# Attention ahead of two MoE layers: float32 scores in the two row halves of the array, one block for both heads' last queries, memory read by token

## The chip, the cores and the metric

The kernel runs on one core of one Trainium2 chip. The metric is the device time of one execution in microseconds, from inputs in HBM to the output in HBM; several executions are timed and the median is given. One more execution is recorded by the hardware profiler, and every line number (L381 is line 381 of the kernel) and every duration of the profile is from it.

## The reference

Attention with a causal mask over 4 batches of 8 heads, 576 tokens of 64 features each, mixed with a read from a memory matrix; then two layers of a feed-forward network over the 2304 tokens.

```
scores = q k^T / 8, masked above the diagonal
a      = exp(scores - max) / (sum + 1e-9)          local = a v
q_p    = phi(q),  phi(x) = max(x, 0) + exp(min(x, 0))
mem    = (q_p M_prev) / (q_p z_prev + 1e-6)        # per head
x      = g * mem + (1 - g) * local,  g = sigmoid(beta) per head
h = x w_in;  x = (h - tanh(h)) w_out                # first layer, 512 -> 2048 -> 512
h = x w2_in; e = h softmax(h); x = (layernorm(e) g_ln) w2_out   # second, 512 -> 1024 -> 512
```

The MoE weights arrive as 64-bit floats; the kernel builds 32-bit ones from the two words of each.

## The kernel before

The work has three stages: attention (class `Attention`), the first layer (`Moe1`) and the second (`Moe2`). Attention treats two heads at once, a pair: the 64 features of one head lie on partitions 0 to 63 and those of the other on 64 to 127. There are 16 pairs. Each token block c has 128 queries that are moved up by 64, so that five blocks of 64, 192, 320, 448 and 576 keys cover a head (`s_mm`, L289).

- q and k of a pair are loaded (L127, L131) and transposed on TensorE (L154, L155).
- **Scores.** The matmuls run in the type float32r, which keeps fewer bits, so q and k are both split into a high and a low part: `q_hi`, `q_lo` (L169), `q_mv` and `k_hi` (L203), `k_lo` (L213), `k_hd`, `k_ld` (L182 on an engine, L184 as a DMA). Each head's q tile stacks the high part on one partition half and the low part on the other, and each k part lies twice, on both halves. One matmul of 128 rows then adds two of the products; KH and KL give the rest.
- **Softmax.** `s_max` (L303, DVE) adds the mask and takes the maximum, `s_exp` (L319, ACT) the exponential with the row sum, `s_inv` (L331, DVE) 1/sum, and `s_norm` (L336, POOL) multiplies by it and by 1 - g.
- **Memory.** phi is made from the untransposed q on DVE and ACT, `f_z` and `f_red` (L241, L245) form the denominator, `f_scale` (L264, POOL) multiplies phi by g and its inverse, `f_t` and `f_ev` transpose it, and `a_mem` (L359) puts the product with M into the PSUM tile X.
- **Product with v.** The probabilities are transposed in four groups a head (`a_t`, L381; `GROUPS` lists key block and query block), copied out of PSUM (`a_ev`, L387), and `a_pv` (L400) adds their product with v to X, one head in each column half of the array. `x_ev` (L415) copies X out and `x_mv` (L420) stores it by DMA into xT, which the first layer reads.

PSUM has three kinds of tile: "S" (two buffers of 1024 columns), "T" (two of 512) and "X" (one of 1024).

**The order of the work is written out by hand.** Inside the manual schedule each engine, and the DMA queue of SyncE, issues in the order of emission. `PROLOGUE` lists the operations of the first two pairs; `PERIOD` is one loop turn, in which `k_t:1` means the transposes of k of the next pair, `s_mm:-1:-:3` block 3 of the head before. A letter names the engine of a copy. `run` goes through them; at the operations called `room`, work on the MoE weights and on xT is let in (`Between`, L633: the class hands out one step at a time). Its first job is added after the first operation that `run` yields, and a job starts by fetching two blocks of raw weights (L688). Once the last scores are done, each attention operation on TensorE is preceded by four matmuls of the first layer (the filler, L589).

```
        for p in range(self.START, NP - last):
            for j, (name, at, engine, part) in enumerate(ops):
                ...
                    if p >= NP and name.startswith(self.ON_PE):
                        next(filler, None)
                    emit(name, i, engine, part)
                yield p, j
```

Of the kernel before, what the change touches and what calls it, by code (L numbers as in the profile page):

```python
# [19 lines left out]
NCB = 4  # L20


class Attention:
# [3 lines left out]
    NPB = 4  # L27

    def __init__(self, ap, sp, ps, tc, q, k, v, M_prev, z_prev, beta, xT, ident):
# [12 lines left out]
        self.NC = S // P + 1  # L42
        assert S == 576 and D == 64
        NC = self.NC

# [4 lines left out]
        self.mask = sp.tile([P, S], F32, tag="mask", name="mask", bufs=1)  # L50
        nc.gpsimd.memset(self.mask, 0.0)
        nc.gpsimd.affine_select(
            out=self.mask[:, S - P :],
            in_=self.mask[:, S - P :],
            compare_op=ALU.is_ge,
            fill=-8.0e9,
            base=0,
            pattern=[[-1, P]],
            channel_multiplier=1,
        )  # L60

        self.nat, self.Qs, self.Pt, self.Md = {}, [], [], []
        for i in range(2):
            t = sp.tile([P, NC, 2, D], F32, tag=f"q{i}", name=f"q{i}", bufs=1)
            nc.gpsimd.memset(t[D:P, NC - 1], 0.0)
            self.nat["q", i] = t

        for name, pool, n, free in (("k", sp, 2, slice(D, P)), ("v", ap, 3, slice(0, D))):
            for i in range(n):
                t = pool.tile([P, NC, 2, D], F32, tag=f"{name}{i}", name=f"{name}{i}", bufs=1)  # L70
                nc.gpsimd.memset(t[free, NC - 1], 0.0)
                self.nat[name, i] = t
        for i in range(2):
            t = ap.tile([P, self.HP, P], F32, tag=f"Md{i}", name=f"Md{i}", bufs=1)
            nc.gpsimd.memset(t, 0.0)
            self.Md.append(t)
        for i in range(4):
            t = sp.tile([P, D + S], F32R, tag=f"Qs{i}", name=f"Qs{i}", bufs=1)
            nc.gpsimd.memset(t[:, 0:D].bitcast(F32), 0.0)
            self.Qs.append(t)  # L80
        self.poff = [P * i * (i + 1) // 2 for i in range(NC)]
        for i in range(self.NPB):
            t = ap.tile([P, self.poff[NC - 1] + S], F32, tag=f"P{i}", name=f"P{i}", bufs=1)
            for c in range(NC - 1):
                o = self.poff[c + 1]
                nc.gpsimd.memset(t[:, o - D : o], 0.0)
            self.Pt.append(t)
        for name in ("x", "zb", "ql", "T", "St", "K", "e", "f", "n", "fT", "mx", "sm", "sc", "pt"):
            setattr(self, name, {})


    def load_gate(self):
# [26 lines left out]

    def _load(self, p, t, src, order, last=0):  # L120
# [3 lines left out]
        full = P * (NC - 1)  # L124
# [21 lines left out]
    def _transposed(self, name, t):  # L146


        nc, NC, S = self.nc, self.NC, self.S
        T = self.ps.tile([P, 1024], F32, tag="S", name=name, bufs=2)  # L150
        full = P * (NC - 1)
# [10 lines left out]
    def q_hi(self, p):  # L162

        self.copy(self.Qs[2 * p % 4][:, self.D :], self.T["q"])

    def q_lo(self, p):
        L = self.ql[p] = self.sp.tile([P, self.S], F32R, tag="ql", name=f"ql{p}", bufs=1)
        H = self.Qs[2 * p % 4][:, self.D :]
        self.nc.vector.tensor_tensor(L, self.T["q"], H.bitcast(F32), ALU.subtract)  # L169

    def q_mv(self, p, i):

        Q = [self.Qs[(2 * p + j) % 4][:, self.D :] for j in range(2)]
        L = self.ql[p]
        a, b = self._half(0)
        out, in_ = ((Q[1][b], Q[0][b]), (Q[0][b], L[a]), (Q[1][a], L[b]))[i]
        self._move(out, in_.bitcast(F32))

    def _move(self, out, in_):

        if self.copy:
            self.copy(out, in_)  # L182
        else:
            self.nc.sync.dma_start(out=out.bitcast(F32), in_=in_)  # L184

    def _half(self, j):

        D = self.D
        a, b = slice(0, D), slice(D, P)
        return (b, a) if j else (a, b)  # L190
# [5 lines left out]
    def k_hi(self, p, j):  # L196

        a, b = self._half(j)
        KH, KL = self.K[2 * p + j] = [
            self.sp.tile([P, self.S], F32R, tag=t, name=f"{t}{p}_{j}", bufs=4)  # L200
            for t in ("KH", "KL")
        ]
        self.copy(KH[a], self.T["k"][a])  # L203

    def k_hd(self, p, j):
        a, b = self._half(j)
        KH, _ = self.K[2 * p + j]
        self._move(KH[b], KH[a].bitcast(F32))

    def k_lo(self, p, j):  # L210
        a, b = self._half(j)
        KH, KL = self.K[2 * p + j]
        self.nc.vector.tensor_tensor(KL[a], self.T["k"][a], KH[a].bitcast(F32), ALU.subtract)  # L213

    def k_ld(self, p, j):
        a, b = self._half(j)
        _, KL = self.K[2 * p + j]
        self._move(KL[b], KL[a].bitcast(F32))


    def f_neg(self, p):
        e = self.e[p] = self.ap.tile([P, self.NC, 2, self.D], F32, tag="fe", name=f"e{p}", bufs=1)
        flat = "p c j d -> p (c j d)"
        self.nc.vector.tensor_scalar_min(e.rearrange(flat), self.nat["q", p % 2].rearrange(flat), 0.0)

    def f_pos(self, p):
        f = self.f[p] = self.ap.tile([P, self.NC, 2, self.D], F32, tag="f", name=f"f{p}", bufs=2)
        flat = "p c j d -> p (c j d)"
        self.nc.vector.tensor_scalar_max(f.rearrange(flat), self.nat["q", p % 2].rearrange(flat), 0.0)

    def f_exp(self, p):
        e = self.e[p].rearrange("p c j d -> p (c j d)")
        self.nc.scalar.activation(e, e, AF.Exp)

    def f_sum(self, p):
        self.eng.tensor_tensor(self.f[p], self.f[p], self.e[p], ALU.add)

    def f_z(self, p):
        b, h0 = divmod(2 * p, self.H)
        z = self.zb[b][:, h0 // 2].unsqueeze(1).broadcast_to([P, self.NC, 2, self.D])  # L240
        self.nc.gpsimd.tensor_tensor(self.e[p], self.f[p], z, ALU.mult)  # L241

    def f_red(self, p):
        n = self.n[p] = self.ap.tile([P, self.NC, 2], F32, tag="fn", name=f"n{p}")
        self.nc.vector.tensor_reduce(n, self.e[p], AX.X, ALU.add)  # L245
# [877 lines left out]
```

## Time and profile before

| | |
|---|---|
| median of three runs | 868.15 us (867.0 to 870.17) |
| the profiled execution | 866.64 us, of which the profile's span is 864.8 us |
| TensorE busy | 837.6 us, 97% of the span |
| DVE, ACT, POOL busy | 625.1, 395.8, 366.7 us |
| mean granted TensorE clock | 0.998 |
| start of the first layer's second product (Y, L616) | 250.47 us |

Busy time of TensorE counts an instruction until its results are out, and the next one starts before that, so 97% doesn't say that the array works at its peak. How much work a stretch of TensorE holds is read from start to start. PEld is TensorE's loading of weights, which overlaps its matmuls. Attention ends, for the purpose of this text, where the first Y of L616 starts.

### The profile page before, as it was taken

How to read it: one execution, taken by the hardware profiler on the slowest of the kernel's cores; microseconds unless marked ns; L12 is line 12 of the kernel's file. 1: busy time of each engine (PE TensorE's matmuls, PEld its weight loads, DVE VectorE, ACT ScalarE, POOL GpSimd, SP SyncE). 2: the span in 40 equal slices, each digit the busy share in tenths (PEclk: the TensorE clock that was granted, in tenths of full speed). 3: DMA queues.
4: the chain of work that ended last, by engine and by line, in shares of the span. 5: the costliest groups of instructions: out<-in, count | busy, mean ns of one | idle time of the engine just before them, and what ended most of it. 6: DMA issues, size and time to landing. Idle time of an engine off the chain costs nothing.

```text
span 864.8 us, 13784 instructions
## 1 busy us (share of the span) xinstructions
PE 837.6 (97%) x5016; PEld 752.5 (87%) x5016; DVE 625.1 (72%) x1215; ACT 395.8 (46%) x843; POOL 366.7 (42%) x453
## 2 busy tenths in 40 slices
PE   4999999999999899999999999999999999999998
PEld 3777777777789899999999999999998888888887
DVE  6888889988657877787777877775787655555553
ACT  5898888888744323323233232332322323323222
POOL 6968787887835333333333333430533111111110
PEclk9999999999999999999999999999999999999999
DMA  6896677565110211212112121220200000000001
GB/s 131 198 207 161 161 183 164 146 146 135 45 52 25 74 60 63 74 50 74 54 69 74 49 74 49 74 70 5 72 27 0 25 25 25 20 19 25 25 25 37
DMA packets 82372, 64.66 MB, mean 75 GB/s; under 512 B 63296, under 2 KB 63552, under 8 KB 82304
## 3 DMA queue, kind: packets, MB, share of 16 engines
q1 hardware_dynamic: 82304, 63.78, 27.3%
q8 instruction: 40, 0.66, 0.3%
q14 instruction: 28, 0.23, 0.1%
HBM read 40.90 MB, written 4.72 MB: 53 GB/s over the span
## 4 chain that ended last, share of the span: by engine, by line
PE 73%; DVE 1%; ACT 1%; issue 0%; ACTq 0%
PE Y L616 23%; PE H L589 23%; PE H L796 11%; PE T L835 2%; PE X L400 1%; PE T L381 1%; PE O9X L865 1%; PE O3X L865 1%; PE O13X L865 1%; PE O11X L865 1%; PE O7X L865 1%; PE O5X L865 1%; PE O1X L865 1%; PE O0X L865 1%; PE O15X L865 1%; PE O16S L865 1%
## 5 line engine op out<-in xcount | busy, mean ns | idle before, releaser
L616 PE MATMUL Y<-G,wo 128*128 128x384 f32 x1152 | 209.3, 337 | 3.0 <-DVE yT L628 2.2
L616 PEld LDWEIGHTS Y<-G,wo 128*128 128x128 f32 x1152 | 202.2, 189 | 3.6 <-ACT cva L732 2.5
L589 PE MATMUL H<-xh,wi 128*128 128x384 f32 x768 | 150.7, 337 | 0.0
L589 PEld LDWEIGHTS H<-xh,wi 128*128 128x128 f32 x768 | 134.8, 188 | 1.3 <-issue 0.8
L600 ACT ACTIVATE t<-H 128x768 f32<-128x768 f32 x48 | 39.1, 814 | 197.4 <-PE H L589 193.0
L750 POOL TENSOR_TENSOR cvw<-cvw,cva 128x512 f32<-128x512 f32 x44 | 56.8, 1291 | 164.6 <-DVE cva L748 121.9
L336 POOL TENSOR_SCALAR P<-P,sm,og 128x192 f32<-128x192 f32 (+4 forms) x160 | 105.8, 673 | 23.1 <-DVE sm L331 19.7
L319 ACT ACTIVATE P<-sc,mx 128x192 f32<-128x192 f32 (+4 forms) x160 | 88.8, 558 | 9.1 <-DVE mx L303 8.6
L796 PE MATMUL H<-w2i,Ys 128*128 128x512 f32 x384 | 90.0, 390 | 0.0
L796 PEld LDWEIGHTS H<-w2i,Ys 128*128 128x128 f32 x384 | 72.0, 188 | 15.0
L601 DVE TENSOR_TENSOR t<-H,t 128x768 f32<-128x768 f32 x48 | 45.9, 957 | 51.6 <-ACT t L600 51.6
L381 PEld LDWEIGHTS T<-ident,P 128*128 128x128 f32 x480 | 52.4, 141 | 35.0 <-DVE mx L303 11.1
L589 PE MATMUL H<-xT,wi 128*128 128x384 f32 x384 | 82.8, 337 | 0.0
L303 DVE CUSTOM_DVE_ANT_0 sc<-S,mask 128x64 f32<-128x64 f32 (+4 forms) x160 | 73.1, 486 | 11.5 <-PE S L289 9.1
L381 PE MATMUL T<-ident,P 128*128 128x128 f32 x480 | 73.2, 281 | 7.6 <-DVE mx L303 6.2
L630 DVE TENSOR_TENSOR yT<-Y,yT 128x384 f32<-128x384 f32 (+1 forms) x126 | 79.0, 683 | 0.0
L603 DVE TENSOR_TENSOR G<-t,G 128x768 fp32r<-128x768 f32 x48 | 46.3, 965 | 42.4 <-ACT G L602 42.4
L824 POOL TENSOR_TENSOR s<-s,nhalf 128x1 f32<-128x1 f32 x18 | 9.9, 551 | 153.3 <-DVE s L823 134.5
L602 ACT CAST G<-t 128x768 fp32r<-128x768 f32 x48 | 40.1, 835 | 63.6 <-DVE t L601 63.6
L589 PEld LDWEIGHTS H<-xT,wi 128*128 128x128 f32 x384 | 67.9, 188 | 0.1
L807 DVE TENSOR_REDUCE s<-H 128x1 f32<-128x1024 f32 x18 | 22.0, 1224 | 59.9 <-PE H L796 59.9
L289 PE MATMUL S<-KH,Qs 128*128 128x256 f32 (+3 forms) x192 | 56.2, 330 | 8.2 <-DVE Qs L182 5.3
(285 smaller groups left out, 1427.0 us busy)
## 6 DMA issues: line engine op xcount, KB each, us to landing
raw<-in_moe_w_in_dram SPq DMA_DIRECT2D x24, 512.0 KB, 3.7
raw<-in_moe_w_out_dram SPq DMA_DIRECT2D x24, 512.0 KB, 3.5
xT<-x SPq DMA_DIRECT2D x16, 288.0 KB, 2.4
out_dram<-ob SPq DMA_DIRECT2D x17, 256.0 KB, 2.0
KH<-KH SPq DMA_DIRECT2D x30, 144.0 KB, 2.8
KL<-KL SPq DMA_DIRECT2D x30, 144.0 KB, 2.7
q<-in_q_dram SPq DMA_DIRECT2D x16, 256.0 KB, 3.7
k<-in_k_dram SPq DMA_DIRECT2D x16, 256.0 KB, 3.6
```

Of the source, the lines that this page charges most:

```text
L289: nc.tensor.matmul(t[:, o + a : o + z], lh, K[:, a:z], start=(i == 0), stop=(i == 1), skip_group_check=True,)
L303: self.nc.vector.tensor_tensor_reduce(out=sc, in0=t[:, o : o + W], in1=self.mask[:, self.S - W :], scale=-0.125, scalar=3.0e38, op0=ALU.ad ...
L319: self.nc.scalar.activation(self._p(n, c), self.sc[c], AF.Exp, bias=self.mx[n][:, c : c + 1], scale=-1.0, accum_out=self.sm[n][:, c : c + 1],)
L336: self.nc.gpsimd.tensor_scalar(d, d, self.sm[n][:, c : c + 1], self.og[:, h : h + 1], ALU.mult, ALU.mult)
L381: nc.tensor.transpose(T[:, at : at + P], Pt[:, col : col + P], self.ident)
L589: nc.tensor.matmul(H[:, f], wi[:, wl, c, f * P : (f + 1) * P], self.x[n][xl][:, c], start=(i == 0), stop=(i == 3 * KD - 1),)
L603: nc.vector.tensor_tensor(G[:, 1], t, G[:, 0].bitcast(F32), ALU.subtract)
L616: nc.tensor.matmul(Y[d][:, 0:NB], wo[:, wl, f, d * P : (d + 1) * P], G[:, gl, f], start=(i == 0), stop=(i == 3 * KF - 1),)
L630: nc.vector.tensor_tensor(y, src, y, ALU.add)
L750: self.eng.tensor_tensor(w, w, a, ALU.add)
L796: nc.tensor.matmul(H[:, nh * 512 : (nh + 1) * 512], Y[:, yl, c, :], w2i[:, wl, c, nh * 512 : (nh + 1) * 512], start=(k == 0), stop=(k == 3 ...
L865: nc.tensor.matmul(O, L[:, ll, f, :], self.w2o[f][:, wl, a : a + w], start=(f == 0 and k == 0), stop=(f == KF - 1 and k == 2),)
```

## The change

Only the attention class changes, and with it the order of its operations; the MoE stages, the filler and the weight conversion stay.

- **Scores** are plain float32 matmuls on the transposed q and k, which are copied out of PSUM whole (`q_ev`, `k_ev`). A head has 64 features, so its matmul uses 64 of the array's 128 rows; head 0 takes rows 0 to 63, head 1 rows 64 to 127. The splits and their moves go. Blocks are no longer moved up: four blocks of 128 queries with 128 to 512 keys (`s_r`).
- **The last 64 queries** of both heads share one tile of 128 partitions (`s_l`): head 0 on partitions 0 to 63, head 1 on 64 to 127, with a mask and a gate of their own. Softmax has nine blocks a pair where it had ten.
- **Memory by token.** phi is made from the transposed q and used as the stationary operand: `m_mm` multiplies it with one tile that holds M of both heads and z as two more columns (`MZ`, 130 columns, g already multiplied in by `m_gate`). `m_eps`, `m_inv` and `m_mul` divide on DVE, and `a_mem` lays the result into X by five transposes.
- **Product with v.** The probabilities are transposed in five groups of four blocks and one of five for the last queries; `PV` lists the products. X has 640 columns, of which the store skips 64.
- **The order.** `PROLOGUE` is empty, the loop starts two periods early, and `PERIOD` is new. M and z of a batch are loaded inside it.

```
+    MW, MS = 130, 176
...
-    def q_hi(self, p):
-    def q_lo(self, p):
-    def q_mv(self, p, i):
-    def k_hi(self, p, j):
-    def k_hd(self, p, j):
-    def k_lo(self, p, j):
-    def k_ld(self, p, j):
+    def q_ev(self, p):
+        t = self.QT[p] = self.sp.tile([P, self.S], F32, tag="QT", name=f"QT{p}", bufs=2)
+        self.copy(t, self.T["q"])
...
+    def load_m(self, p):
...
+            nc.sync.dma_start(
+                out=t[rows, :, P + j : P + j + 1],
+                in_=self.z[b].rearrange("(c j) (d o) -> j d c o", j=2, o=1)[j],
+            )
...
+    def m_mm(self, p):
...
+        for i in range(self.NC):
+            at = min(P * i, self.S - P)
+            o = self.MS * i
+            nc.tensor.matmul(
+                R[:, o : o + self.MW], f[:, at : at + P], self.MZ[b % 2][:, c, :], start=True, stop=True,
+                skip_group_check=True,
+            )
...
+    def s_r(self, p, c):
+        nc, D = self.nc, self.D
+        Q, K = self.QT[p], self.KT[p]
+        if c == 1:
+            t = [
+                self.ps.tile([P, 512], F32, tag="T", name=f"S{p}_{c}{j}", bufs=2)
+                for j in range(2)
+            ]
+        else:
+            S = self.ps.tile([P, 1024], F32, tag="S", name=f"S{p}_{c}", bufs=2)
+            t = [S[:, 0:512], S[:, 512:1024]]
...
+        for r, o in ((c, 0),) if c > 1 else ((1, 0), (0, 256)):
+            w = P * (r + 1)
+            for j in range(2):
+                rows = slice(j * D, (j + 1) * D)
+                s = self.St[p, 2 * r + j] = t[j][:, o : o + w]
                 nc.tensor.matmul(
+                    s, Q[rows, P * r : P * r + P], K[rows, 0:w], start=True, stop=True,
                     skip_group_check=True,
                 )
+    def s_l(self, p):
...
+        for a, z in ((0, full), (full, S)):
+            for j in range(2):
+                rows = slice(j * D, (j + 1) * D)
+                nc.tensor.matmul(
+                    t[rows, a:z], Q[rows, full:S], K[rows, a:z], start=True, stop=True,
+                    skip_group_check=True,
+                )
...
+    PV = [
+        [(0, 0, 512, (0, 1), (0, 0))],
+        [(1, 128, 384, (2, 3), (0, 0)), (3, 384, 128, (2, 3), (384, 384))],
+        [(2, 256, 256, (4, 4), (0, 256))],
+        [(kb, 576, 64, (5, 5), (P * kb, P * kb + 64)) for kb in range(5)],
+    ]
...
     PERIOD = """
+        load_q:2:- f_exp:0:- s_exp:0:-:5 s_r:0:-:3 s_max:0:-:0 s_norm:-1:-:5 a_pv:-2:-:3
+        s_max:0:-:1 s_norm:-1:-:6 s_max:0:-:2 s_exp:0:-:0 x_mv:-3:- a_pv:-2:-:2
+        s_max:0:-:6 s_norm:-1:-:8 s_exp:0:-:1 s_max:0:-:7 s_norm:-1:-:7 a_pv:-2:-:1
+        a_pv:-2:-:0 s_max:0:-:3 m_gate:1:- s_l:0:- a_t:-1:-:2 s_exp:0:-:2 s_norm:-1:-:1
+        s_exp:0:-:4 a_t:-1:-:5 f_sum:0:p s_norm:-1:-:0 s_max:0:-:8 s_exp:0:-:7 load_k:2:-
+        load_m:2:- a_ev:-1:v:5 x_ev:-2:a a_t:-1:-:4 k_t:1:- a_ev:-1:a:2 f_neg:1:v
+        s_exp:0:-:3 s_exp:0:-:6 a_t:-1:-:1 a_ev:-1:a:4 s_eps:0:-:1 m_mm:0:- s_inv:0:-:1
+        a_mem:-1:- a_t:-1:-:3 k_ev:1:a room:0:-:2 a_ev:-1:v:1 f_pos:1:v m_eps:0:-
+        s_norm:0:-:2 s_norm:0:-:3 m_inv:0:- a_t:-1:-:0 s_norm:0:-:4 s_exp:0:-:8 m_mul:0:-
+        room:0:-:0 a_ev:-1:v:3 room:0:-:1 a_ev:-1:a:0 s_eps:0:-:0 q_t:2:- s_inv:0:-:0
+        s_r:1:-:2 s_max:1:-:5 load_v:1:- s_r:1:-:1 s_max:1:-:4 q_ev:2:a
     """
...
+        first = max(at for _, at, _, _ in ops)
+        for p in range(self.START or -first, NP - last):
...
+                    if self.scores == 0 and name.startswith(self.ON_PE):
                         next(filler, None)
```

More of the change, by code (lines that the diff above doesn't have):

```diff
@@ L42, in __init__ @@
         self.NC = S // P + 1
+        self.done, self.scores = 0, self.NP * (self.LAST + 1)
         assert S == 576 and D == 64
         NC = self.NC
+        full = self.full = P * (NC - 1)
         self.ap, self.sp, self.ps = ap, sp, ps
[L50 to L68, printed above, removed]
+        self.mask = sp.tile([P, full], F32, tag="mask", name="mask", bufs=1)
+        self.maskL = sp.tile([P, S], F32, tag="maskL", name="maskL", bufs=1)
+        for mask, rows, n in (
+            (self.mask, slice(0, P), P),
+            (self.maskL, slice(0, D), D), (self.maskL, slice(D, P), D),
+        ):
+            w = mask.shape[1]
+            nc.gpsimd.memset(mask[rows], 0.0)
+            nc.gpsimd.affine_select(
+                out=mask[rows, w - n :],
+                in_=mask[rows, w - n :],
+                compare_op=ALU.is_ge,
+                fill=-8.0e9,
+                base=0,
+                pattern=[[-1, n]],
+                channel_multiplier=1,
+            )
+        self.nat, self.MZ = {}, []
+        for name, pool, n, free in (
+            ("q", sp, 2, slice(D, P)), ("k", sp, 2, slice(D, P)), ("v", ap, 3, slice(0, D))
+        ):
             for i in range(n):
@@ new lines, in a_ev, with a_pv @@
+    def a_ev(self, p, g):
+        T = self.pt[p, g]
+        w = T.shape[1]
+        pt = self.ap.tile([P, w], F32, tag=f"pt{w}", name=f"pt{p}_{g}", bufs=5 if w == 512 else 1)
+        self.copy(pt, T)
+        self.pt[p, g] = pt
+    PV = [
[4 more added lines that the diff above has]
+    ]
+    def a_pv(self, p, i):
+        D = self.D
+        v = self.nat["v", p % 3]
+        for kb, q0, w, gs, at in self.PV[i]:
+            for j in range(2):
+                self.nc.tensor.matmul(
+                    self.X[j * D : (j + 1) * D, q0 : q0 + w],
+                    v[:, kb, j, :],
+                    self.pt[p, gs[j]][:, at[j] : at[j] + w],
+                    start=False, stop=False, skip_group_check=True,
+                )
@@ L475, in run @@
+        room:0:-:0 a_ev:-1:v:3 room:0:-:1 a_ev:-1:a:0 s_eps:0:-:0 q_t:2:- s_inv:0:-:0
+        s_r:1:-:2 s_max:1:-:5 load_v:1:- s_r:1:-:1 s_max:1:-:4 q_ev:2:a
+    """
+    ON_PE = ("q_t", "k_t", "m_mm", "s_r", "s_l", "a_mem", "a_t", "a_pv")
     def run(self, filler):
```

385 lines of the change are left out of this document (137 added, 248 removed), and 7 rows, old and new, of the table GROUPS.

## The prediction

> **What bounds the kernel now.** I first asked for the busy time of each engine by stretches, then for TensorE's instructions in order of time over one head pair, then for the waits.
>
> The first view gives, for each stretch (start:end, its length), the busy time of each engine with its instruction count in brackets. The third stretch runs from the transposes of the features of pair 2 to those of pair 15, so it holds 13 periods of the loop.
>
> ```profile
> core 0: us, PE busy (x) PEld busy (x) DVE busy (x) ACT busy (x) POOL busy (x), PEclk, DMA share, GB/s
> 0.00:10.00 10.00, 2.63 (x10) 1.83 (x10) 3.42 (x5) 3.21 (x4) 7.80 (x39) 1.00 0.54 117
> 10.00:20.00 10.00, 6.14 (x24) 5.04 (x25) 9.23 (x21) 7.70 (x16) 4.69 (x5) 1.00 0.70 146
> 46.40:226.20 179.80, 173.98 (x1357) 136.29 (x1356) 156.30 (x434) 156.52 (x425) 142.08 (x216) 1.00 0.64 156
> ```
>
> A period takes 179.8 / 13 = 13.83 us. TensorE is busy for 97% of it; DVE and ACT for 12.0 us each, POOL for 10.9. So TensorE sets the pace from about 30 us on, and the first 20 us are a chain of single steps in which it worked 8.8 us. Attention ends here, after one last idle stretch of 1.43 us (in brackets, with what ended it):
>
> ```profile
> 231.39 0.66 PE L381 MATMUL T<-ident,P 128*128 128x128 f32 x4 [1.43 <-DVE mx L303]
> ...
> 249.67 0.97 PE L589 MATMUL H<-xT,wi 128*128 128x384 f32 x4
> 250.47 5.71 PE L616 MATMUL Y<-G,wo 128*128 128x384 f32 x32
> ```
>
> From 250.5 us to the end at 864.8 us the two MoE layers run, and nothing in the change touches them. So the question is how long it takes until that Y can start. Now one period on TensorE, from Tf to Tf (start, length of the merged group, line, how many instructions):
>
> ```profile
> 129.69 0.60 PE L154 MATMUL Tf<-ident,f 128*128 128x128 f32 x4
> ...
> 130.88 0.98 PE L400 MATMUL X<-pt,v 128*64 128x128 f32 x8
> 131.78 0.66 PE L381 MATMUL T<-ident,P 128*128 128x128 f32 x4
> ...
> 133.42 0.98 PE L400 MATMUL X<-pt,v 128*64 128x256 f32 x8
> 134.33 0.87 PE L381 MATMUL T<-ident,P 128*128 128x128 f32 x6
> 135.14 0.88 PE L400 MATMUL X<-pt,v 128*64 128x64 f32 x8
> 135.94 1.15 PE L381 MATMUL T<-ident,P 128*128 128x128 f32 x8
> 136.85 0.52 PE L289 MATMUL S<-KH,Qs 128*128 128x256 f32 x2
> ...
> 137.57 0.77 PE L400 MATMUL X<-pt,v 128*64 128x256 f32 x8
> 138.27 0.41 PE L289 MATMUL S<-KH,Qs 128*128 128x320 f32 x1
> ...
> 140.06 0.60 PE L154 MATMUL Tq<-ident,q 128*128 128x128 f32 x4
> ...
> 140.60 0.60 PE L381 MATMUL T<-ident,P 128*128 128x128 f32 x4
> 141.04 1.14 PE L359 MATMUL X<-fT,Md 128*128 128x256 f32 x4
> 142.01 0.66 PE L381 MATMUL T<-ident,P 128*128 128x128 f32 x4
> ...
> 143.01 0.60 PE L154 MATMUL Tf<-ident,f 128*128 128x128 f32 x4
> ```
>
> Instructions overlap in their pipeline, so I price by start to next start, not by length. This undisturbed period is 13.32 us of pure work; the mean is 0.5 us longer. Three prices come out of it. A float32 matmul: the memory product moves 256 + 320 columns from 141.04 to 142.01, 0.97 us, or 1.68 ns a column. A transpose: five of q from 140.06 to 140.60, eight of P from 135.94 to 136.85, so 0.108 to 0.114 us; I take 0.115 with the slow first one of a group. And the product with v, whose two heads use the two column halves of the array: its four groups take 0.90 + 0.91 + 0.80 + 0.70 = 3.31 us for 1600 columns of each head (the widths in GROUPS). One head after the other would be 3200 x 1.68 = 5.38 us, both at once 2.69. The halves do run together; the 0.62 us left over are about 0.155 us a group for filling and emptying.
>
> **The change, part by part.** TensorE, per pair, afterwards:
>
> - Transposes: five each of q and k as now, none of the features, 25 of the probabilities in place of 30, and five that lay the memory part into X: 40 x 0.115 = 4.60 us.
> - Product with v: again 1600 columns a head, 2.69, now as one run of four groups, so one fill of 0.155 and some for the 20 small matmuls of 64 columns: 2.90.
> - Scores of the first 512 queries (s_r): 512 + 384 + 256 + 128 = 1280 columns a head in float32 with 64 rows, one head in each row half. No row shows row halves. The bounds: both at once, 1280 x 1.68 = 2.15; one after the other, 4.30. The nearest row is that of the column halves, which overlap, so I take 2.15 + 0.15.
> - Last 64 queries (s_l): 576 columns, both heads into the two partition halves of one tile: 0.97 to 1.94, I take 0.97 + 0.15.
> - Memory product by token (m_mm): five of 130 columns, 650 x 1.68 = 1.09.
> - Three further changes between full array, halves and quarters, 0.1 each: 0.3.
>
> Sum: 4.60 + 2.90 + 2.30 + 1.12 + 1.09 + 0.30 = 12.3 us against 13.32. The price of a change of array shape is in this view of the waits (46 to 230 us; total, times, longest):
>
> ```profile
> PEld T L381 <- DVE mx L303: 9.0, 9, 1.5
> PEld X L400 <- issue: 6.4, 39, 0.2
> ```
>
> Before 39 of the products with v the weight load stood for 0.16 us and waited for no engine. The Trainium skill, "TensorEngine Tiling (Array Packing)", Key Properties, says that a change of tiling mode drains the array. That row fits the rule, and against this change it says that two more modes come in; but the order written out has row halves, column halves, quarters and full array once each per period, four changes where there are eight now, so by the rule the sum would hold 4 x 0.16 = 0.64 us for them, where mine holds 0.155 + 0.15 + 0.15 + 0.30 = 0.76.
>
> The other engines must now stay under 12.3 us. The rows that carry what goes (busy total, mean ns of one):
>
> ```profile
> L236 DVE TENSOR_TENSOR f<-f,e 128x640 f32<-128x640 f32 x13 | 25.4, 1955 | 0.0
> L303 DVE CUSTOM_DVE_ANT_0 sc<-S,mask 128x576 f32<-128x576 f32 x32 | 24.1, 753 | 2.9 <-PE S L289 1.8 <-ACT P L319 0.3
> L213 DVE TENSOR_TENSOR KL<-Tk,KH 64x576 fp32r<-64x576 f32 x32 | 24.1, 753 | 4.1 <-ACT KH L203 3.4
> L245 DVE TENSOR_REDUCE n<-e 128x10 f32<-128x640 f32 x16 | 13.0, 815 | 0.1
> L169 DVE TENSOR_TENSOR ql<-Tq,Qs 128x576 fp32r<-128x576 f32 x16 | 11.7, 730 | 0.9 <-ACT Qs L164 0.8
> L387 DVE COPY pt<-T 128x448 f32<-128x448 f32 x17 | 10.6, 623 | 2.5 <-PE T L381 1.8
> L203 ACT CAST KH<-Tk 64x576 fp32r<-64x576 f32 x32 | 20.3, 636 | 0.5
> L271 ACT COPY fT<-Tf 128x576 f32<-128x576 f32 x16 | 10.3, 646 | 0.0
> L319 ACT ACTIVATE P<-sc,mx 128x576 f32<-128x576 f32 x32 | 24.8, 776 | 0.1
> L241 POOL TENSOR_TENSOR e<-f,zb 128x640 f32<-128x640 f32 x16 | 24.9, 1555 | 11.2 <-DVE f L236 9.9 <-DMA zb<-in_z_prev_dram 1.2
> L264 POOL TENSOR_TENSOR f<-f,n 128x640 f32<-128x640 f32 x16 | 20.1, 1259 | 0.4
> ```
>
> DVE loses f_sum (25.4 / 16 = 1.6 us a pair), the two k remainders (1.5), the row sums (0.8) and the q remainder (0.7). It gains, at 1.4 ns a column from the copy of 448, one more column-wide eviction (512 + 512 + 640 in place of 448 + 384, 1.2 us) and the memory division (640 columns out of PSUM at the 1.27 ns of the q remainder, 0.8, and two small ones, 0.4). 12.0 - 4.6 + 2.4 = 9.8. ACT loses one of two casts of k (0.6) and the features' copy (0.65), and evicts 3 x 512 columns of P in place of some 2340: 0.9 us at the 1.12 ns of that copy. 12.0 - 2.15 = 9.9. POOL loses the two products with z and 1/n (1.55 + 1.26) and takes f_sum over (576 columns, 1.4): 10.9 - 1.4 = 9.5. The softmax's rows count as unchanged: nine instructions over 3136 columns, not ten over 3200, and the one at 576 columns costs 753 on DVE and 776 on ACT as before. All three sit under TensorE with 2.4 us or more to spare, which is the cover under which I cost their edits at nothing. It was 1.3 us for DVE and ACT before, and the mean period held 0.5 us of waits, the longest of them behind DVE (9.0 us above). I take 0.25 us of waits, so 12.5 us a period; the bounds are 12.3 with none and 13.2 with twice the old waits.
>
> The order written out by hand for the first two pairs goes; the loop now begins two periods early, with nothing ahead of it. Rows of the start, and last one of the list of DMA issues (each of so many KB, median us from issue to landing):
>
> ```profile
> 6.75 0.62 SPq L127 DMA_DIRECT2D q<-in_q_dram  x1
> 12.28 0.82 PE L289 MATMUL S<-KH,Qs 128*128 128x256 f32 x2 [5.25 <-DVE Qs L182]
> 36.40 0.95 SPq L688 DMA_DIRECT2D raw<-in_moe_w_in_dram  x2
> ...
> q<-in_q_dram SPq DMA_DIRECT2D x16, 256.0 KB, 3.7
> ```
>
> Now the first scores wait for the hi/lo halves until 12.28. Those go, but something else is late next. The first step after the loop's first operation adds the weight conversion, and that fetches at once: two issues of 512 KB, here at 36.40, will stand on SP right behind q of pair 0 and ahead of k, beta, memory, z and q of pair 1. And on TensorE the scores of pair 0 stand behind the transposes of q of pair 1. That load is issued at 6.75 now. Two weight issues (0.95) come ahead of it, two z loads replace the one broadcast: about 8, and a q load takes 3.7 us to land. So the first scores start near 12.3 again, the second group ends at 13. From there period 0 is bound by ACT (the 9.9 without evictions of P, 8.2, and the first chain through it, so 9.5 us), period 1 by ACT and DVE with evictions (10.5), then 14 full periods, then pair 15's last transposes and pair 14's products with v among eleven filler steps of the first MoE, then pair 15's products. A filler step of four matmuls is 0.80 us (249.67 to 250.47). So:
>
> 13.0 + 9.5 + 10.5 + 14 x 12.5 + (2.9 + 3.5 + 11 x 0.8 + 1.7 for the remaining weight and x steps, which made TensorE wait 1.43 us in the row of 231.39) + 2.9 + 0.8 = 229.6 us, against 250.5. That is 20.9 us less. The profiled execution took 866.64 us around its span of 864.8, so 845.7; it lies 1.5 us under the median of the runs (868.15), so I forecast 847 us.
>
> DMA loses five copies a pair between partition halves and gains one small store: the share of 0.64 above falls, and no load is late for that.
>
> **The rivals.**
>
> *Row halves run one after the other.* Nothing in the trace shows two row halves at once; what it shows is column halves. In float32 each head would then add 1856 x 1.68 = 3.12 us a pair: 14 x 3.12 + 2 in period 1, since TensorE then has 12.4 us of work there, = 45.7, so 893 us, slower. It decides as soon as more than 13.83 - 12.5 = 1.3 us of the 3.12 stay unhidden. Against it: 3.31 us in place of 5.38 for the column halves, in the same type and through the same weight loads.
>
> *They overlap only in part.* With their fill, column halves gain 5.38 / 3.31 = 1.63, not 2. If row halves do no better in each of their four groups, scores take 6.24 / 1.63 = 3.83 in place of 3.42: 0.4 x 14 = 6, so 853. If only s_l fails, since its two heads write one bank, 0.97 x 14 = 14, so 861. "TensorEngine Tiling (Array Packing)", Gotcha 1, of the Trainium skill states that different row tiles cannot use one PSUM bank at a time; by that rule it is this second case, and no row here shows it. In s_r each head has its own bank.
>
> *Waits take the gain.* The two large PSUM buffers now serve seven tiles a period (q, k, two of s_r, s_l, m_mm, the last group of P), five before, and s_r(1) takes both small ones at once, behind two evictions. The row of 9.0 us is such a wait: transposes of P stand until DVE has read the scores in the buffer. If each such circle costs what the worst did (1.5 us), the period is 12.3 + 1.5 = 13.8, as before, and only the shorter start and end are left: 14 x 1.3 = 18 back, 865 us, no change. For it: more tiles on the same buffers. Against it: the slack of 2.4 us on each engine.
>
> **How the numbers follow.** The forecast has 0.60, the partial overlap 0.13, the waits 0.12, the one after the other 0.15. The unknown start (up to 5 us if k and q of pair 1 come behind the megabyte of weights) and the period (12.3 to 13.2: -3 to +10) give the likeliest case 842 to 860 of its own. Lower lies only a start under 11 us with no waits, 835. The range 835 to 868 leaves out the serial case and a little on each side. What a measurement of this kernel can tell from no change is 0.5%, 4.3 us. Faster than 863.8: the forecast, the partial overlap nearly whole, a third of the waits: 0.60 + 0.11 + 0.04 = 0.75. Within it: 0.08, from the waits and a poor overlap. Slower: 0.15 + 0.02 = 0.17.
>
> **What would show each step.** Right: two matmuls of s_r starting within some ns of each other and 512 columns of both heads taking 0.86 us, not 1.72; a distance of 12.5 us between the q transposes of two pairs; DVE and ACT under 10 us in it; first scores near 12 us with the weight loads on SP ahead of k; Y starting near 230 us. Wrong: TensorE still 97% busy but with periods over 15 us (serial halves), or below 92% busy with waits on evictions (buffers); or a different time after Y starts, which would mean that the change reaches into the MoE layers.

## The result, and the profile after

The changed kernel takes 843.54 us (842.33 to 843.84) against 867.81 us for the kernel before, measured beside it: 0.9713 of its time, with a 95% interval of 0.9692 to 0.9735. The forecast was 847 us. The profiled execution took 842.33 us around a span of 840.5 us. Of all executions in this text one, of the last experiment's kernel, took 4651.94 us where the other four took 834.4 to 836.16; it doesn't count in the ratio, and nothing here explains it.

Y (now L579) starts at 226.37 us, 24.1 us earlier than before. From there to the end it is 840.5 - 226.37 = 614.1 us, where it was 864.8 - 250.47 = 614.3: the MoE layers are untouched, and the whole gain lies in attention.

First view of the changed kernel: busy time by stretches. The first ends at the first scores (`s_r`, L265), the second is 13 periods long, the third ends at Y.

```profile
core 0: us, PE busy (x) PEld busy (x) DVE busy (x) ACT busy (x) POOL busy (x), PEclk, DMA share, GB/s
0.00:14.90 14.90, 3.85 (x15) 2.78 (x15) 2.56 (x8) 2.77 (x4) 6.07 (x22) 1.00 0.73 167
45.63:201.65 156.02, 156.02 (x1444) 114.11 (x1445) 116.07 (x373) 124.21 (x333) 116.38 (x169) 1.00 0.40 97
201.65:226.37 24.72, 19.58 (x126) 15.65 (x123) 13.34 (x19) 7.52 (x13) 7.62 (x9) 0.86 0.21 67
```

In the 13 periods TensorE has no idle moment at all: 156.02 / 13 = 12.00 us each, where it was 13.83. DVE is busy for 116.07 / 13 = 8.9 us of a period, ACT for 9.6, POOL for 9.0. The three stages to look at are thus the start, in which TensorE works 3.85 us of 14.90, the period, which is TensorE's work and nothing else, and the end, in which it is idle for 5.1 us and its granted clock falls to 0.86.

One period on TensorE, in order of time (start, length of the merged group, line, count):

```profile
110.89 1.19 PE L279 MATMUL S_L<-KT,QT 64*64 64x512 f32 x8
112.01 0.66 PE L375 MATMUL T<-ident,P 128*128 128x128 f32 x4
...
114.47 1.28 PE L216 MATMUL R<-MZ,f 128*128 128x130 f32 x10
115.59 0.71 PE L357 MATMUL X<-ident,xm 128*128 128x128 f32 x5
...
117.65 2.43 PE L265 MATMUL S<-KT,QT 64*128 64x384 f32 x16
120.01 2.96 PE L399 MATMUL X<-pt,v 128*64 128x64 f32 x36
122.89 1.19 PE L279 MATMUL S_L<-KT,QT 64*64 64x512 f32 x8
```

Start to start: `s_r` 2.36 us, product with v 2.88, `s_l` 1.12 (110.89 to 112.01), memory by token 1.12, and 2.46 + 2.06 = 4.52 for the 40 transposes (112.01 to 114.47, 115.59 to 117.65). Their sum is 12.00.

Whether the two row halves run at once shows in the same view, cut to a window of 15 ns for the first row and of 12 ns for the second; the count is then of the matmuls under way in that window:

```profile
117.65 0.59 PE L265 MATMUL S<-KT,QT 64*128 64x384 f32 x2
...
122.89 0.65 PE L279 MATMUL S_L<-KT,QT 64*64 64x512 f32 x2
```

Both heads' first matmuls of `s_r` are under way by 117.660, and both of `s_l` by 122.905, each within 15 ns of the start of its group. In `s_r` 1280 columns a head at 1.68 ns are 2.15 us, and 2.36 are taken; one head after the other would be 4.30.

The start, on TensorE, and on the queue of SyncE (SPq), which issues the loads:

```profile
9.92 1.11 PE L172 MATMUL Tk<-ident,k 128*128 128x128 f32 x4 [4.33 <-DMA k<-in_k_dram]
...
13.67 1.09 PE L172 MATMUL Tq<-ident,q 128*128 128x128 f32 x4 [2.43 <-DMA q<-in_q_dram]
...
14.90 4.11 PE L265 MATMUL S<-KT,QT 64*128 64x384 f32 x16
...
24.32 2.43 PE L265 MATMUL S<-KT,QT 64*128 64x384 f32 x16 [0.56 <-DVE xm L235]
...
33.62 2.43 PE L265 MATMUL S<-KT,QT 64*128 64x384 f32 x16
```

```profile
2.27 1.10 SPq L651 DMA_DIRECT2D raw<-in_moe_w_in_dram  x2
3.41 0.61 SPq L146 DMA_DIRECT2D k<-in_k_dram  x1
...
6.01 1.87 SPq L120 DMA_DIRECT2D MZ<-in_M_prev_dram  x1
...
9.90 0.62 SPq L146 DMA_DIRECT2D q<-in_q_dram  x1
```

The weights are issued ahead of k; k waits behind them, and q of pair 1, for which TensorE stands last before the scores, is issued at 9.90. The end:

```profile
209.18 0.80 PE L375 MATMUL T<-ident,P 128*128 128x128 f32 x4 [4.03 <-ACT pt L382]
...
212.92 1.09 PE L375 MATMUL T<-ident,P 128*128 128x128 f32 x4 [1.02 <-DVE pt L382]
213.94 4.07 PE L399 MATMUL X<-pt,v 128*64 128x64 f32 x36
217.94 1.66 PE L552 MATMUL H<-xh,wi 128*128 128x384 f32 x8
```

Between the last operations of attention stands no matmul of the first layer (L552). All of them follow from 217.94 on, 8.4 us until Y, and TensorE waits 4.03 and 1.02 us for evictions before that.

### The profile page after: what moved, and what is told of

Same layout as the page of the kernel before. It is cut to its first block, busy times and chain, and to the rows that moved or that the text cites. A ratio compares the mean times of both kernels' runs of the same rounds, so it can differ in the third digit from the quotient of the medians.

```text
span 840.5 us, 13466 instructions
## 1 busy us (share of the span) xinstructions
PE 816.9 (97%) x5096; PEld 725.9 (86%) x5096; DVE 572.8 (68%) x1139; ACT 351.9 (42%) x727; POOL 326.5 (39%) x374
## 4 chain that ended last, share of the span: by engine, by line
PE 93%; DVE 4%; DMA 1%; ACT 1%; SPq 0%; issue 0%; ACTq 0%
PE Y L579 23%; PE H L552 22%; PE H L759 12%; PE T L375 5%; PE X L399 5%; PE S L265 5%; PE R L216 2%; PE S_L L279 2%; PE T L798 2%; PE X L357 1%; PE Tk L172 1%; PE Tq L172 1%; DMA k<-in_k_dram 1%; PE O3X L828 1%; PE O13X L828 1%; PE O11X L828 1%
## 5 line engine op out<-in xcount | busy, mean ns | idle before, releaser
L579 PE MATMUL Y<-G,wo 128*128 128x384 f32 x1152 | 209.3, 337 | 3.0 <-DVE yT L591 2.2
L579 PEld LDWEIGHTS Y<-G,wo 128*128 128x128 f32 x1152 | 202.1, 189 | 3.6 <-ACT cva L695 2.5
L552 PE MATMUL H<-xh,wi 128*128 128x384 f32 x768 | 149.3, 336 | 0.0
L552 PEld LDWEIGHTS H<-xh,wi 128*128 128x128 f32 x768 | 135.1, 188 | 0.8 <-issue 0.8
L335 POOL TENSOR_SCALAR P<-P,sm,og 128x256 f32<-128x256 f32 (+3 forms) x128 | 81.0, 641 | 8.7 <-DVE sm L326 5.9
L552 PE MATMUL H<-xT,wi 128*128 128x384 f32 x384 | 82.4, 336 | 0.0
L311 ACT ACTIVATE P<-sc,mx 128x256 f32<-128x256 f32 (+3 forms) x128 | 70.5, 552 | 7.0 <-DVE mx L289 7.0
L552 PEld LDWEIGHTS H<-xT,wi 128*128 128x128 f32 x384 | 68.1, 188 | 0.0
L289 DVE CUSTOM_DVE_ANT_0 sc<-S,mask 128x384 f32<-128x384 f32 (+3 forms) x128 | 54.0, 486 | 7.4 <-PE S L265 7.3
L805 ACT CAST L<-T 128x512 fp32r<-128x512 f32 x36 | 19.4, 590 | 80.4 <-PE T L798 80.4
L375 PE MATMUL T<-ident,P 128*128 128x128 f32 x320 | 47.7, 280 | 5.1 <-ACT pt L382 4.0
L399 PE MATMUL X<-pt,v 128*64 128x64 f32 (+4 forms) x576 | 48.4, 324 | 0.0
```

The source lines that it names most:

```text
L289: self.nc.vector.tensor_tensor_reduce(out=sc, in0=s, in1=mask, scale=-0.125, scalar=3.0e38, op0=ALU.add, op1=ALU.min, accum_out=self.mx[p] ...
L311: self.nc.scalar.activation(t, self.sc.pop((p, i)), AF.Exp, bias=self.mx[p][:, i : i + 1], scale=-1.0, accum_out=self.sm[p][:, i : i + 1],)
L335: self.nc.gpsimd.tensor_scalar(d, d, self.sm[p][:, i : i + 1], og, ALU.mult, ALU.mult)
L375: nc.tensor.transpose(T[:, P * i : P * i + P], t, self.ident)
L399: self.nc.tensor.matmul(self.X[j * D : (j + 1) * D, q0 : q0 + w], v[:, kb, j, :], self.pt[p, gs[j]][:, at[j] : at[j] + w], start=False, st ...
L552: nc.tensor.matmul(H[:, f], wi[:, wl, c, f * P : (f + 1) * P], self.x[n][xl][:, c], start=(i == 0), stop=(i == 3 * KD - 1),)
```

## The experiments

Each starts from the changed kernel. Times without a range are of one execution.

**Both heads in the same row half.** Head 1's `s_r` reads rows 0 to 63 too, so its scores are those of head 0; the work is the same.

```
-                rows = slice(j * D, (j + 1) * D)
+                rows = slice(0, D)
```

> The changed kernel, but both heads' s_r matmuls read rows 0 to 63, so head 1's scores of the first 512 queries are those of head 0. The number and shape of all instructions stay. Theory (the gain stands on the two row halves working at once): the two matmuls of a block now run one after the other, s_r takes 4.3 to 4.5 us a pair where it took 2.36, the period goes from 12.00 to 14.1, and the time from 843.5 to about 843.5 + 14 x 2.1 + 1 = 874 us, slower than before the change (867.8). Rival (the halves are a by-thing, the gain comes from fewer transposes and fewer changes of shape): the period stays within 0.3 us of 12.0 and the time under 849.

Measured: 877.7 us, beside 865.84 us for the kernel before. Two rows of TensorE in order of time, one period apart, and ahead of them the same group cut to a window of 0.1 us:

```profile
112.92 0.59 PE L265 MATMUL S<-KT,QT 64*128 64x384 f32 x1
...
112.92 4.58 PE L265 MATMUL S<-KT,QT 64*128 64x384 f32 x16
...
127.08 4.58 PE L265 MATMUL S<-KT,QT 64*128 64x384 f32 x16
```

Now one matmul is under way in the first 0.1 us, not two. The period is 14.16 us, 2.16 us longer, which is the 2.15 us of one more head, and the kernel is slower than before. The overlap of the row halves is therefore worth the whole gain of the change and some 12 us more (877.7 - 865.84), and TensorE's work sets the period. What the memory by token and the shared block for the last queries are worth was not run alone.

**More TensorE work.** The four large transposes of q and of k are done twice.

```
             nc.tensor.transpose(mv[:, c, :], t[:, c], self.ident)
+            nc.tensor.transpose(mv[:, c, :], t[:, c], self.ident)
```

> The changed kernel with each of the four large transposes of q and of k issued twice, eight more instructions a pair on TensorE and no other work. Theory (TensorE sets the period with no slack): 8 x 0.109 = 0.87 us more a period, 12.9, and 16 x 0.87 = 13 to 14 us more in all, 857. Rival (a circle of PSUM buffers or another engine sets 12.00 us): TensorE takes up the work in part, period under 12.4, under 850.

Measured: 853.73 us. Again one period of TensorE:

```profile
112.42 2.43 PE L266 MATMUL S<-KT,QT 64*128 64x384 f32 x16
...
125.30 2.43 PE L266 MATMUL S<-KT,QT 64*128 64x384 f32 x16
```

12.88 us: eight transposes cost 0.88, 0.11 each, all of it in the period. Y starts at 239.36, 13.0 us later. Nothing else absorbs TensorE work.

**More changes of array shape.** `s_l` moves between two groups of the product with v, and a group of transposes between two others: seven changes a period in place of four, with the same matmuls.

```
-        s_max:0:-:1 s_norm:-1:-:6 s_max:0:-:2 s_exp:0:-:0 x_mv:-3:- a_pv:-2:-:2
+        s_max:0:-:1 s_norm:-1:-:6 s_max:0:-:2 s_exp:0:-:0 x_mv:-3:- a_pv:-2:-:2 s_l:0:-
...
-        a_pv:-2:-:0 s_max:0:-:3 m_gate:1:- s_l:0:- a_t:-1:-:2 s_exp:0:-:2 s_norm:-1:-:1
+        s_max:0:-:3 m_gate:1:- a_t:-1:-:2 a_pv:-2:-:0 s_exp:0:-:2 s_norm:-1:-:1
```

> The changed kernel with another order on TensorE and the same instructions: s_l stands between the second and third group of the product with v, and the first transposes of P between its third and fourth, so that a period has seven changes of array shape where it had four. Theory (a change costs about 0.15 us): 12.00 + 3 x 0.15 = 12.45 us a period, 6 to 7 us more in all. Rival (a change costs nothing when the next weights are there): 12.0 to 12.1 us, within 2 us.

Measured: 846.41 us, beside 841.98 us for the changed kernel on the same chip.

```profile
108.50 2.43 PE L265 MATMUL S<-KT,QT 64*128 64x384 f32 x16
...
120.95 2.43 PE L265 MATMUL S<-KT,QT 64*128 64x384 f32 x16
```

The period is 12.45 us (some are 12.53): 0.45 / 3 = 0.15 us a change. Y starts 5.6 us later, while the times of the two kernels differ by 4.4. The price is the size of the 0.16 us which the prediction read from the weight load ahead of the products with v, but that row is no measure of it: in the changed kernel it reads `PEld X L399 <- issue: 14.9, 41, 0.8` (30 to 200 us), which is 0.36 us each, and the price is still 0.15. By that price the step from eight changes to four is an estimated 0.6 of the 1.83 us that a period lost.

**The splits' work put back where it was.** On DVE the three subtractions and on ACT the two copies that made the low and high parts follow `q_ev` and `k_ev` again and read PSUM; nothing uses what they write. For k:

```
+        L = self.sp.tile([P, self.S], F32, tag="kl", name=f"kl{p}", bufs=1)
+        for j in range(2):
+            rows = slice(j * self.D, (j + 1) * self.D)
+            self.nc.vector.tensor_tensor(L[rows], self.T["k"][rows], t[rows], ALU.subtract)
+        for j in range(2):
+            h = self.sp.tile([P, self.S], F32, tag="kh", name=f"kh{p}_{j}", bufs=1)
+            self.nc.scalar.copy(h, self.T["k"])
```

> The changed kernel, with the evictions and subtractions of the old split put back as idle work on scratch tiles: one subtraction of 128x576 and two of 64x576 a pair on DVE (2.1 us), two copies of 128x576 on ACT (1.1 us). DVE goes from 8.9 to 11.0 us a period, ACT from 9.6 to 10.7. Theory (TensorE alone sets the 12.00 us, the other engines are cover): the period stays under 12.15 us, the time within 3 us of the changed kernel's. Rival (that TensorE waits for nothing comes from the slack that the splits left behind): waits come back, 12.4 to 13.2 us a period, 6 to 17 us more.

Measured: 887.89 us, 46 more than the changed kernel's 841.98 and far more than the rival's 6 to 17. The first theory, that work on DVE and ACT is free as long as each engine's sum stays under the period, falls. TensorE over one period, then DVE in its middle:

```profile
114.95 0.63 PE L384 MATMUL T<-ident,P 128*128 128x128 f32 x4 [1.20 <-DVE pt L391]
...
116.63 1.57 PE L274 MATMUL S<-KT,QT 64*128 64x384 f32 x12 [0.33 <-DVE xm L244]
118.68 1.13 PE L274 MATMUL S<-KT,QT 64*128 64x512 f32 x4 [0.48 <-DVE mx L298]
...
131.34 1.61 PE L274 MATMUL S<-KT,QT 64*128 64x384 f32 x12 [0.33 <-DVE xm L244]
```

```profile
112.56 1.52 DVE L196 TENSOR_TENSOR kl<-Tk,KT 64x576 f32<-64x576 f32 x2 [0.82 <-ACT KT L192]
114.11 0.69 DVE L391 COPY pt<-T 128x512 f32<-128x512 f32 x1
```

This period is 14.71 us (others are up to 15.43). DVE is busy for only 98.51 us of 133.00 (57 to 190 us), 10.9 in a period of this length. Its k subtractions first wait 0.82 us for ACT, then work 1.52, and the eviction of a group of P stands behind both; TensorE waits 1.20 us for that buffer, and twice more further on.

**The same work in DVE's and ACT's idle places.** Three subtractions of the same sizes and two copies, now from SBUF, stand where DVE waits for `s_l` and ACT for the first transposes of P.

```
+    def d_v(self, p):
...
+        self.nc.vector.tensor_tensor(L, Q, K, ALU.subtract)
+        for j in range(2):
+            rows = slice(j * self.D, (j + 1) * self.D)
+            self.nc.vector.tensor_tensor(L[rows], Q[rows], K[rows], ALU.subtract)
+    def d_a(self, p):
...
+        self.nc.scalar.copy(h, self.KT[p])
...
-        a_pv:-2:-:0 s_max:0:-:3 m_gate:1:- s_l:0:- a_t:-1:-:2 s_exp:0:-:2 s_norm:-1:-:1
-        s_exp:0:-:4 a_t:-1:-:5 f_sum:0:p s_norm:-1:-:0 s_max:0:-:8 s_exp:0:-:7 load_k:2:-
-        load_m:2:- a_ev:-1:v:5 x_ev:-2:a a_t:-1:-:4 k_t:1:- a_ev:-1:a:2 f_neg:1:v
+        a_pv:-2:-:0 s_max:0:-:3 d_v:0:- m_gate:1:- s_l:0:- a_t:-1:-:2 s_exp:0:-:2 s_norm:-1:-:1
+        s_exp:0:-:4 a_t:-1:-:5 f_sum:0:p s_norm:-1:-:0 s_max:0:-:8 s_exp:0:-:7 d_a:0:- load_k:2:-
+        load_m:2:- a_ev:-1:v:5 x_ev:-2:a d_a:0:- a_t:-1:-:4 k_t:1:- a_ev:-1:a:2 f_neg:1:v
```

> The changed kernel with the same idle work as split_load (one subtraction of 128x576 and two of 64x576 on DVE, two copies of 128x576 on ACT a pair), but reading the copied q and k in SBUF and placed where these engines wait: on DVE behind the last s_max of s_r, in front of its wait of 2.14 us for s_l; on ACT ahead of and behind the copy of X, in front of its waits of 0.51 and 0.99 us. Theory (the place in the engine's queue decides, not its total): the period stays under 12.3 us and the time within 5 us of the changed kernel's 842. Rival (the total decides: 11.0 us of DVE and 10.7 of ACT cannot be fitted into 12 us with these dependencies): 13 us a period or more, 857 or above, as in split_load with its 14.7.

Measured: 856.97 us, beside 867.45 us for the kernel before. That is 15 us above the changed kernel's 841.98, where at most 5 were expected; about half of it lies ahead of the third `s_r` (at 41.19 us for 33.62). The periods behind it (41.19 to 191.82 us) differ among themselves, from 12.00 to 13.24 us, and take 12.55 in the mean. Two neighbours (columns as in the first view), and what TensorE waits for in the longer one:

```profile
116.68:128.68 12.00, 12.00 (x111) 8.81 (x111) 10.80 (x33) 10.76 (x29) 8.48 (x13) 1.00 0.37 88
103.67:116.68 13.01, 12.22 (x112) 8.79 (x111) 12.37 (x33) 11.03 (x29) 11.89 (x17) 1.00 0.45 106
```

```profile
112.46 0.66 PE L172 MATMUL Tk<-ident,k 128*128 128x128 f32 x4 [0.79 <-DVE mx L301]
```

In the first, DVE carries 10.80 us and ACT 10.76, as much as with the splits put back, and the period is 12.00 us to the hundredth. So such a sum need not cost anything, and the place of the work counts. But this holds for two of the twelve periods alone, and the second shows where it ends: the same DVE instructions take 12.37 us, and the maximum over `s_l` comes late. DVE in the two periods, then POOL:

```profile
108.83 2.78 DVE L199 TENSOR_TENSOR ql<-QT,KT 64x576 f32<-64x576 f32 x2
...
121.75 1.66 DVE L199 TENSOR_TENSOR ql<-QT,KT 64x576 f32<-64x576 f32 x2
```

```profile
109.09 1.90 POOL L217 TENSOR_TENSOR f<-f,e 128x576 f32<-128x576 f32 x1
...
119.64 1.42 POOL L217 TENSOR_TENSOR f<-f,e 128x576 f32<-128x576 f32 x1
```

In the longer period POOL has more to do (11.89 us against 8.48), and its sum of two tensors falls on the time of DVE's subtractions. Both become longer: 2.78 us for 1.66, 1.90 for 1.42. That this overlap is what makes the period longer is read from these rows and was not tried alone, nor was the part of the source (PSUM or SBUF) in the difference from the run before.

**The filler at the end.** In `run` the filler runs where `self.scores == 0`. Now that the loop's own last turns finish the scores, this count has already been set to -1, by the lines that open the first layer, when pair 15's operations come.

```
-                    if self.scores == 0 and name.startswith(self.ON_PE):
+                    if self.scores <= 0 and name.startswith(self.ON_PE):
```

> The changed kernel, but the filler of the first MoE is let in when the count of open scores is zero or less; the main loop sets that count to -1 at once, so that the test for exactly zero never held and all 48 filler matmuls ran behind the last product with v, from 217.94 us. Theory (the end of attention lost the filler's cover): TensorE's idle 4.03 and 1.02 us and the lower clock of 0.86 in the last 25 us go, as 48 matmuls at 0.174 to 0.2 us fill them; Y starts at 219 to 221 us in place of 226.4 and the time is 836 to 838. Rival (the wait is set by the weight conversion ahead of the copies on ACT and DVE, the filler only stands in front of it): Y starts within 2 us of 226.4 and the time stays at 842 or above.

Measured: 837.19 us (836.96 to 839.62), 0.9672 [0.9651, 0.9693] of before. TensorE at the end:

```profile
211.91 0.97 PE L552 MATMUL H<-xh,wi 128*128 128x384 f32 x4 [1.85 <-DVE pt L382]
...
214.21 0.63 PE L375 MATMUL T<-ident,P 128*128 128x128 f32 x4 [0.20 <-ACT pt L382]
...
222.10 2.08 PE L579 MATMUL Y<-G,wo 128*128 128x384 f32 x11
```

The stretch in the columns of the first view:

```profile
201.65:226.37 24.72, 22.66 (x168) 17.46 (x163) 17.40 (x22) 10.68 (x20) 9.83 (x10) 1.00 0.22 68
```

The first layer's matmuls stand between the transposes, the waits shrink from 5.05 to 2.05 us, the granted clock stays at 1.00, and Y starts at 222.10 us, 4.3 earlier (219 to 221 was expected). The interval still touches the changed kernel's, 0.9692 to 0.9735, so the step is shown by the trace more than by the times.

**The weights after the first loads.**

```
-            (rooms, lambda p: True, lambda: loader.steps(2)),
+            (rooms, lambda p: p >= 0, lambda: loader.steps(2)),
```

> The changed kernel, but the job of weight conversion is added two periods later, so that its two fetches of 512 KB are issued behind the loads of the first two pairs. Theory (k and q of the first pairs come late because they are queued behind a megabyte of weights): k's transposes start near 6 us in place of 9.92, those of q of pair 1 near 12.5 in place of 13.67, the first scores at 13.5 to 14 in place of 14.90, and the time falls by 1 to 1.5 us to about 842.3. Rival (the issue of 16 loads one after the other on SP sets the start, not the bytes): k's transposes come earlier, the first scores stay within 0.4 us of 14.9, no change of time.

Measured: 840.88 us, 0.9705 [0.9690, 0.9719] of before, which the interval doesn't tell from the changed kernel's 0.9713. The trace tells more. TensorE, then SyncE's queue:

```profile
5.66 1.12 PE L172 MATMUL Tk<-ident,k 128*128 128x128 f32 x4
...
12.89 3.78 PE L265 MATMUL S<-KT,QT 64*128 64x384 f32 x14
```

```profile
5.43 0.61 SPq L120 DMA_DIRECT2D MZ<-in_M_prev_dram  x1
```

k comes 4.3 us earlier, the scores 2.0, Y 1.9 (224.51). The scores gain less than k because q of pair 1 still stands behind the loads of M and z, though the issue that took 1.87 us behind the weights now takes 0.61.

**All of it together.** Filler and weights as above, and M and z loaded one turn later (`load_m:1`, `m_gate:0`). The changed kernel ran beside it once more.

> The changed kernel with the filler let in (as in fill_fixed), the weight conversion added two periods later (as in raw_later), and M, z and the gate of a batch loaded one period later, behind q and k of the next pair, with m_gate at its own pair. Theory (each loss at the two ends is separate, the steady period is full): q of pair 1 is issued near 4.2 us in place of 9.9, the first scores start at 9 to 10 us in place of 14.9, the middle keeps its 12.00 us, the end is that of fill_fixed (4.3 us less); together 9 to 10 us less than the changed kernel, a ratio to before of 0.960 to 0.962. Rival (an earlier start is given back, because period 0 and 1 wait for k and v of the next pairs or for M): first scores before 11 us, but at most 6 us less than the changed kernel, a ratio of 0.964 or above.

> The changed kernel once more, so that the variants have it on their own chip: 0.971 of the time of before, within the interval 0.969 to 0.974.

Measured: 835.76 us, 0.9636 [0.9611, 0.9661] of before; the changed kernel 841.98 us, 0.9695 [0.9659, 0.9731]. The expected 9 to 10 us are not reached: 6.2 us lie between the two, and the rival, at most 6 us and a ratio of 0.964, is nearly met. The scores start at 8.61 us, 6.3 earlier than in the changed kernel, but Y at 220.29, no more than the sum of the two edits alone. The rest is given back at once, in TensorE's wait for the product with M, which follows POOL's gating of it:

```profile
17.77 2.30 PE L216 MATMUL R<-MZ,f 128*128 128x130 f32 x10 [3.30 <-POOL sm L322]
```

```profile
14.45 1.04 POOL L135 TENSOR_TENSOR MZ<-MZ,g 128x512 f32<-128x512 f32 x1 [8.57 <-DVE g L103]
```

**The gate ahead of the first exponential,** so that POOL isn't late with M.

```
-                    if i == 0 and name == "m_gate":
+                    if i == 0 and name == "s_exp" and part == [5]:
```

> The kernel of best, with the gate (an exponential on ACT and five small operations on DVE) issued ahead of the first exponential of pair 0, not in the middle of period 0. Theory (in best the gate's late place held up POOL until 14.45, so f_sum and with it m_mm until 17.77, while TensorE stood 3.3 us): m_mm starts near 15.5 us, the third s_r near 29 in place of 31.2, the time is 2 us less than that of best, a ratio to before of 0.961. Rival (M's own arrival sets it): m_mm within 0.5 us of 17.8, same time as best.

> The kernel of best once more, so that best2 has it on its own chip: a ratio to before of 0.961 to 0.966.

Measured: 835.32 us, 0.9633 [0.9618, 0.9647], against 835.72 us, 0.9642 [0.9625, 0.9659], for the kernel above beside it: no difference that these tell. The rival's time came true, but not its reason, that M's own arrival sets the start. POOL and then TensorE:

```profile
12.06 1.04 POOL L135 TENSOR_TENSOR MZ<-MZ,g 128x512 f32<-128x512 f32 x1 [6.19 <-DVE g L103]
```

```profile
16.65 0.75 PE L172 MATMUL Tk<-ident,k 128*128 128x128 f32 x4 [3.63 <-DVE mx L289]
...
17.71 2.50 PE L216 MATMUL R<-MZ,f 128*128 128x130 f32 x10
```

The gating is done 2.4 us earlier, but the wait has moved: the gate's steps on DVE now stand among the first maxima (11.52 to 14.48 us, 2.32 of them in `12.16 2.32 DVE L109 COPY ogL<-og 64x4 f32<-64x4 f32 x2`), the transposes of k wait 3.63 us for them, and the product with M starts at 17.71 as before.

## Why the prediction was right, and where it wasn't

The direction, the mechanism of the period and the size held. Its chain, term by term, beside the starts of `s_r` and Y:

| term | predicted | measured |
|---|---|---|
| to the first scores (12.3 to their start, 13.0 to the end of their second group) | 13.0 | 14.9 (start) |
| period 0 | 9.5 | 9.4 (24.32 - 14.90) |
| period 1 | 10.5 | 9.3 (33.62 - 24.32) |
| 14 periods | 175.0 | 168.0 (201.65 - 33.62) |
| end | 20.6 by its terms, 21.6 in the total | 24.7 (226.37 - 201.65) |
| Y | 229.6 | 226.4 |

The terms written out add up to 228.6, not 229.6: those of the end, 2.9 + 3.5 + 8.8 + 1.7 + 2.9 + 0.8, are 20.6. By its own terms the forecast is 846 us.

- **Row halves at once: right.** 2.36 us for the 2.30 that were put down, and the run with both heads in one half shows the price of the rival, 2.16 us a period for `s_r` alone. The rival's 893 us had `s_l` serial as well, 3.12 a pair; that part was not tried.
- **Partial overlap: fell.** `s_r` and `s_l` take 2.36 + 1.12 = 3.48 us, for 3.42 with the overlap put down and 3.83 with a partial one. On `s_l`, whose two heads write one bank, the Trainium skill, "TensorEngine Tiling (Array Packing)", Gotcha 1, says that different row tiles cannot access one PSUM bank at the same time. The trace doesn't agree for two tiles that write different partitions of a bank: both matmuls are under way within 15 ns, and 576 columns take 1.12 us, where one after the other would be 1.94.
- **TensorE's terms: right but for one.** Product with v 2.88 for 2.90, memory 1.12 for 1.09, transposes 4.52 for 4.60, `s_l` 1.12 for 1.12. The "three further changes" at 0.3 measured nothing of their own: four changes a period at 0.15 us were already in the fills of `s_r`, `s_l` and the product with v. They were counted twice.
- **Waits: 0.25 us put down, 0.00 measured.** The circles through the two PSUM buffers never close late. With the 0.3 above and the smaller differences this is the half microsecond by which 12.5 was too long, 7 us over 14 periods.
- **"All three sit under TensorE with 2.4 us or more to spare": the sums held within 0.9 us, the inference didn't.** They measured 8.9, 9.6 and 9.0 us for 9.8, 9.9 and 9.5. But the runs show that the spare sum is not cover by itself: 10.9 us on DVE cost 2.7 us a period in one place of its queue, and 10.8 us nothing in two periods of another. That the edits were free is by these two runs a matter of the order written out as much as of the sums; the order of the changed kernel itself was not varied alone.
- **Start: weights ahead of k, right; mis-sized by 2.6 us.** First scores at 14.9 for 12.3. The issue of q of pair 1 was put at 8 us and came at 9.90, since one issue in the queue took 1.87 us, not 0.6, behind the weights.
- **Period 0: the number met by luck.** ACT was to bind it with 9.5 us. It is busy for 7.81 of the 9.42 us and TensorE for 8.12; TensorE's first group of `s_r` lasts 4.11 us where the next ones last 2.43, and its last wait ends with DVE (0.56 us at 24.32). Why the first group is so long stays open.
- **Period 1:** ACT and DVE did not bind it (8.3 us each, with TensorE busy throughout); 9.3 for 10.5.
- **End: wrong.** The step "pair 14's products with v among eleven filler steps" took the filler to run. It doesn't: the count that it tests is -1 by then. With the test mended the end measures 222.10 - 202.14 = 20.0 us (its `s_r` at 130.13 and six more periods of 12.00) for the 20.6 of the terms, so 4.8 us of the 24.7 are this, a lower clock included. The line was there to be read before.

The errors had both signs, +1.9 and +3.1 us (+4.1 against the end's own terms) against -7.0 and -1.3. That 847 came within 4 us of the measured time is in part luck.

## What to carry to other kernels

Where one engine has no idle time, price each operation by start to next start: this gave the period to 4% (12.5 us for 12.00). Here a change of the array's shape cost about 0.15 us, so grouping operations of one shape was a gain of its own. Don't take an engine's free time as cover: look at what stands behind the added work in that engine's queue and who waits for it. When a prologue or a loop's bounds change, read again every condition that counts what is left to do, and the order in the DMA queue ahead of the first load.

## What the runs showed of the hardware that was not expected

- Two row tiles that write different partitions of one PSUM bank run at once in float32 (begun within 15 ns, 1.12 us for 576 columns of both heads).
- DVE and POOL delay each other when both work on two tensors in SBUF: 2.78 us for 1.66 and 1.90 for 1.42. The Trainium skill, "SBUF — State Buffer", Who interferes with whom, gives the two engines one shared pair of ports under an exclusive lock. The rows agree in size: the first of the two subtractions would end at 108.83 + 0.83 = 109.66, 0.57 us after POOL's start, and POOL takes 0.48 longer.
- The mean granted clock of 0.86 over the last 24.7 us is half the clock for 6.8 us, behind the idle time of 4.03 us. The second row is of the kernel with all of it together (columns as in the first view):

```profile
209.50:216.33 6.83, 5.81 (x42) 4.55 (x42) 4.47 (x8) 1.64 (x4) 1.08 (x1) 0.50 0.39 120
...
209.13:212.55 3.42, 3.42 (x13) 3.23 (x14) 2.49 (x4) 1.90 (x3) 0.00 (x0) 0.50 0.14 46
```

The last product with v, begun in the first of them, takes 217.94 - 213.94 = 4.00 us, where it takes 2.88 in the period. With the filler alone the clock stayed at 1.00 behind an idle time of 1.85 us, but with all of it together it was halved behind the same 1.85 us. So the length of the idle time alone doesn't decide it; what else does stays open. One of the eight executions of the changed kernel has a mean clock of 0.998 and takes 838.88 us, where the others have 0.992 to 0.994 and take 841.49 to 843.84.
